# A gated feed-forward kernel on one core: where the ninth group's last mean stands on ScalarE

## The chip, the core and the metric

The kernel runs on one core of one Trainium2 chip. The metric is the device time of one execution in microseconds (us); the median of three executions is given, and one more execution was taken with the hardware profiler. Four engines of the core matter here: TensorE (PE in the profile) does matrix products into accumulation banks, ScalarE (ACT) does activation functions from a loaded table, VectorE (DVE) does element-wise arithmetic, and SyncE (SP) issues the transfers. Every engine works through its own queue of instructions.

## The reference

An attention block without a softmax feeds a gated feed-forward block, all in fp32:

```python
kv  = einsum('bhsd,bhse->bhde', k, v)          # 8 batches, 8 heads, 576 rows, 64 columns
o   = einsum('bhsd,bhde->bhse', q, kv)
x   = o / sqrt(mean(o*o, -1) + 1e-6) * g_norm  # RMS norm per row and head
x   = x.transpose(0, 2, 1, 3).reshape(4608, 512)
h   = x @ w_in                                 # 512 -> 2048
g   = h * erf(log1p(exp(-abs(h))) + maximum(h, 0))   # h * erf(softplus(h))
out = g @ w_out                                # 2048 -> 512
```

## The kernel before, in words

**Groups.** The 4608 rows are worked in nine groups of 512 rows. Groups 0 to 7 are the first 512 rows of each batch; the ninth group (T = 8, `T == B` in the code) collects the last 64 rows of all eight batches, whose attention products were computed along the way and kept in `x_last`. Groups 0 and 1 take a plain fp32 path; from group 2 on every product is made of three products of cut operands ("forms": high part, low part and a mix of both, lines 367 to 390).

**Periods.** From group 2 on the work runs in periods (loop variable `m`, 8 to 36). A period takes a quarter of a group's 2048 hidden columns: `T, b = divmod(m, 4)`. In a period TensorE makes four *hidden products* (function `hidden`, i = 0 to 3, x times a block of w_in) and then four *result products* (function `result`, j = 0 to 3, the gated values of the period before times w_out, added to a running sum `e`). Each of these eight is twelve matmuls of 128x512 (line 434): eight into a bank `n_ps`, then four into a bank `m_ps`. The two banks come from three pairs that go round (`banks`), so product number k writes the pair that product k - 3 used, and has to wait until that one was read.

**What frees a pair.** After a hidden product, ScalarE copies `n_ps` to `h` (line 754), VectorE adds `m_ps` (line 419, called from `add`), and ScalarE takes softplus of the sum (line 756). After a result product, VectorE adds `n_ps` to `e` (line 414) and then `m_ps` (line 419). Each of these also is an instruction in a queue, in the order in which the program is written: the schedule is written out by hand (`manual_schedule`), and no planner moves anything.

**After the four hidden products** ScalarE takes erf of the four softplus tiles in two halves (line 760). Softplus, erf, and the pair Ln and Exp lie in three different tables; a switch is a table load, put in by `exp_ln_table` (line 103), `softplus_table` (line 106) or, for erf, at the activation itself (line 760). After result product 1 VectorE multiplies h by erf's result in two halves (line 772).

**The next group's pieces.** While period `m` runs, it also carries one quarter of the attention of group T + 1, cut into six pieces, and `places` says where each goes: place 0 is ahead of the period's first product, places 1 to 4 follow hidden products 0 to 3, places 5 to 8 follow result products 0 to 3. For the ninth group the six pieces are: nothing, `square` (ScalarE, line 314), nothing, `mean`, `norm` and `split`. `mean` is one fp32 product of 128x512 on TensorE (line 333), then on ScalarE the table of Ln and Exp, Ln (line 340), Exp (341), Square (342) and, if `table` is true, softplus's table again (106). `norm` is three VectorE instructions (348, 351, 360). `split` cuts the normalized tile into its three forms: one ScalarE instruction (385) and two on VectorE (388, 389); they go into `x_forms` of the ninth group, which period 32's first hidden product reads.

The ninth group's four quarters are carried by periods 28 to 31 (T = 7). Periods 28 to 30 have `places = (0, 0, 0, 5, 6, 7)`, so the mean follows result product 0 and stands behind erf on ScalarE. Period 31, the last, has `(0, 0, 0, 2, 4, 5)`: its mean follows hidden product 1.

Of the kernel before, what the change touches and what calls it, by code (L numbers as in the profile page):

```python
# [58 lines left out]
def kernel(  # L59
# [45 lines left out]
    def softplus_table():  # L105
        nc.scalar.preload_act_table_set("softplus")  # L106
# [311 lines left out]
    def add(out_, ps):  # L418
        nc.vector.tensor_tensor(out=out_, in0=ps, in1=out_, op=ALU.add)  # L419
# [44 lines left out]
    NB = FC // BATCH  # L464
# [73 lines left out]
    def load_parts(which, n):  # L538


        pool = w_out_p if which == "out" and len(w_seq["out"]) > BATCH else w_in_p
        for _ in range(n):
            if w_seq[which]:
                key = w_seq[which].pop(0)
                t = pool.tile([P, 3, G], FP32, name=f"w_{which}_parts", tag="w")
                nc.sync.dma_start(out=t, in_=w_kept[key])
                w_now.setdefault(key, []).append(t)
# [124 lines left out]
    def hidden(T, f):  # L672

        w = w_now["in", f].pop(0).rearrange("p i (c f) -> p i c f", c=KC).bitcast(FP32R)
        return product(lambda form, c: w[:, form, c], lambda form, c: x_forms[T][:, form, c])

    def part(h, half):
        return h[:, :, half * 2 * P : half * 2 * P + 2 * P]

    def cut_upper(h, half):  # L680

        t = late_r.tile([P, 3, BATCH, 2 * P], FP32R, name=f"g_forms{half}")
        upper(part(h, half), t[:, 0])
        return t

    def cut_lower(h, half, t):
        lower(part(h, half), *(t[:, i] for i in range(3)))

    def result(T, b, j, g, w):

        ps = product(
            lambda form, f: g[j // 2][:, form, f, j % 2 * P : j % 2 * P + P],
            lambda form, f: w[f][:, form],
        )
        if b == 0:
            es[j] = acc.tile([P, DM], FP32, name="e", tag="e")
            nc.vector.tensor_scalar(
                out=es[j], in0=ps[0], scalar1=SHIFT - 1.0, scalar2=None, op0=ALU.mult
            )
        else:  # L700
            add_scaled(es[j], ps[0], SHIFT - 1.0)
        add(es[j], ps[1])
        if b == NB - 1:
            store(T, j, es.pop(j))
# [5 lines left out]
    for m in range(first_batch, batches + 1):  # L710
        T, b = divmod(m, NB)
        todo = []
        if T + 1 < NG:
            todo = list(attention(T + 1, b))
            if b == 0:
                side = late_r if T % 2 == FIRST % 2 else late
                x_forms[T + 1] = side.tile([P, 3, KC, G], FP32R, name=f"x_forms{(T + 1) % 2}")

        def piece():
            if todo:  # L720
                todo.pop(0)()


        places = (0, 2, 3, 5, 6, 8)
        if T + 1 == B:
            places = (0, 0, 0, 2, 4, 5) if b == NB - 1 else (0, 0, 0, 5, 6, 7)
        elif T + 2 == B and b == NB - 1:
            places = (0, 2, 3, 5, 6, 7)

        def pieces(place):  # L730
            while todo and places[-len(todo)] <= place:
                todo.pop(0)()

        def fetch(place):
            for which in FETCH[place].split():
                load_parts(which, 1)

        pieces(0)
        g, done = g_next, len(g_next)
        g_next = []  # L740
        if m < batches:
            h = wide.tile([P, BATCH, G], FP32, name="h", tag="h")
            s = gate_r.tile([P, BATCH, G], FP32, name="s", tag="s")
        for i in range(BATCH):
            if m < batches:
                n_ps, m_ps = hidden(T, b * BATCH + i)
            fetch(i)
            if i == 0:
                for half in range(done, 2):
                    g.append(cut_upper(old_h, half))  # L750
            if done <= i < 2:
                cut_lower(old_h, i, g[i])
            if m < batches:
                nc.scalar.activation(h[:, i], n_ps, AF.Copy, scale=SHIFT - 1.0)  # L754
                add(h[:, i], m_ps)
                nc.scalar.activation(s[:, i], h[:, i], AF.Softplus)  # L756
            pieces(i + 1)
        if m < batches:
            for i in range(2):
                nc.scalar.activation(part(s, i), part(s, i), AF.Erf)  # L760
            if len(todo) < 3:
                softplus_table()
        T2, b2 = divmod(m - 1, NB)
        w = [w_now["out", b2 * BATCH + f].pop(0).bitcast(FP32R) for f in range(BATCH)]
        for j in range(J):
            result(T2, b2, j, g, w)
            fetch(BATCH + j)
            if j == 1 and m == batches - 1:
                cut_lower(h, 0, g_next[0])

            for half in range(2) if j == 1 and m < batches - 1 else (j,) if j < 2 and m == batches - 1 else ():
                nc.vector.tensor_tensor(  # L772
                    out=part(h, half), in0=part(h, half), in1=part(s, half), op=ALU.mult
                )
            if j == 0 and m == batches - 1:
                g_next.append(cut_upper(h, 0))
            pieces(BATCH + 1 + j)
        old_h = h
# [33 lines left out]
```

## Time and profile before

| | |
|---|---|
| median of 3 executions | 965.39 us (965.13 to 966.09) |
| span of the profiled execution | 966.1 us |
| busy, TensorE | 944.1 us, 98% |
| busy, VectorE | 728.1 us, 75% |
| busy, ScalarE | 616.7 us, 64% |
| table loads at line 106 | 45 of 1283 ns |
| period 31 | from 835.08 us to 862.46 us of the span |

A line of the timeline gives the start in us, the duration in us, the engine, the line of the code, the operation with the tile it writes and those it reads, the number of merged instructions, and in brackets the idle time of the engine before it and who ended it. A line of the table of waits gives the engine and tile that waited, the releaser, the total in us, how often, and the longest. The table of windows gives for a stretch of the span the busy time of each engine with the number of instructions, then the clock that TensorE was granted (1.00 is full), the share of the DMA engines, and GB/s. Durations of matmuls are modelled and overlap the next one; the distance from start to start is the safer measure.

### The profile page before, as it was taken

To read this page: it belongs to the slowest core of one execution; us is meant where nothing else is said; L and a number is where in the kernel's file an instruction comes from. 1 tells how busy PE (TensorE), PEld (TensorE's weight loads), DVE (VectorE), ACT (ScalarE), POOL (GpSimd) and SP (SyncE) were. 2 spreads that over 40 slices of the span, in tenths; PEclk is the share of its full clock that TensorE was granted. 3 is DMA by queue.
4 is the path that set the end of the run, shared out by engine and by line. 5 is a ranking of instruction groups with operands and counts; after the bars stand their busy time and mean duration, and the time that the engine had idled before them with its cause. 6 is when DMAs were issued, how large, how long until landed. Compare 5 with 4: busy or idle time off the path is not lost.

```text
span 966.1 us, 11759 instructions
## 1 busy us (share of the span) xinstructions
PE 944.1 (98%) x4328; PEld 679.6 (70%) x4328; DVE 728.1 (75%) x1036; ACT 616.7 (64%) x824; POOL 2.4 (0%) x10
## 2 busy tenths in 40 slices
PE   6999999999999999999999999999999999989998
PEld 4444444444478887888788878887888787768886
DVE  2979857766277777888888887888787877758667
ACT  3889865686576666666666666666666666665552
POOL 0000000000000000000000000000000000000000
PEclk9999999999999999999999999999999999999999
DMA  9856507889289986998689876987796769756972
GB/s 263 254 163 210 177 1 291 308 317 361 89 302 352 377 290 199 301 382 302 230 270 379 304 282 217 362 334 272 238 353 256 265 228 360 288 211 241 384 275 70
DMA packets 101464, 259.76 MB, mean 269 GB/s; under 512 B 44064, under 2 KB 58400, under 8 KB 101408
## 3 DMA queue, kind: packets, MB, share of 16 engines
q1 hardware_dynamic: 99776, 256.73, 74.7%
q10 hardware_dynamic: 1568, 2.29, 0.8%
q8 instruction: 34, 0.56, 0.2%
q14 instruction: 22, 0.18, 0.0%
q0 software_dynamic: 64, 0.00, 0.0%
HBM read 224.40 MB, written 34.60 MB: 268 GB/s over the span
## 4 chain that ended last, share of the span: by engine, by line
PE 89%; ACT 4%; DVE 3%; DMA 2%; issue 0%; SPq 0%; DVEq 0%
PE n_ps L434 41%; PE m_ps L434 20%; PE o_ps L471 10%; PE h_ps L614 9%; PE se_ps L307 3%; PE kv_ps L279 2%; PE qt_ps L301 2%; DMA w_out_parts<-w_out 1%; DMA v_sb<-in_v_dram 1%; PE ms_ps L333 1%; DMA q_last<-in_q_dram 1%; PE ms_ps L328 1%; PE ms_ps L329 1%; PE kv_ps L306 1%; DVE h L772 0%; ACT w_e L203 0%
## 5 line engine op out<-in xcount | busy, mean ns | idle before, releaser
L434 PE MATMUL n_ps<-x_forms,w_in_parts 128*128 128x512 f32 x896 | 234.2, 403 | 1.3 <-DVE e L414 1.2
L434 PE MATMUL n_ps<-w_out_parts,g_forms 128*128 128x512 f32 x928 | 232.1, 392 | 2.8 <-ACT h L754 2.2
L434 PEld LDWEIGHTS n_ps<-w_out_parts,g_forms 128*128 128x128 f32 x928 | 174.7, 188 | 41.7 <-ACT h L754 2.6
L434 PEld LDWEIGHTS n_ps<-x_forms,w_in_parts 128*128 128x128 f32 x896 | 166.7, 188 | 46.6 <-issue 9.6
L756 ACT ACTIVATE s<-h 128x512 f32<-128x512 f32 x112 | 71.0, 634 | 176.6 <-DVE h L419 176.6
L434 PE MATMUL m_ps<-w_out_parts,g_forms 128*128 128x512 f32 x464 | 125.0, 392 | 0.0
L419 DVE TENSOR_TENSOR h<-m_ps,h 128x512 f32<-128x512 f32 x112 | 77.1, 689 | 61.5 <-ACT h L754 46.2
L434 PE MATMUL m_ps<-x_forms,w_in_parts 128*128 128x512 f32 x448 | 120.1, 390 | 0.0
L614 PE MATMUL h_ps<-xT,w_in_sb 128*128 128x512 f32 x256 | 115.1, 593 | 0.7 <-DVE w_in_sb L228 0.6
L471 PE MATMUL o_ps<-w_out_sb,h_sb 128*128 128x512 f32 x224 | 101.3, 596 | 0.0
L434 PEld LDWEIGHTS m_ps<-w_out_parts,g_forms 128*128 128x128 f32 x464 | 87.7, 189 | 18.3
L434 PEld LDWEIGHTS m_ps<-x_forms,w_in_parts 128*128 128x128 f32 x448 | 84.1, 188 | 17.6
L419 DVE TENSOR_TENSOR e<-m_ps,e 128x512 f32<-128x512 f32 x116 | 80.3, 692 | 18.0 <-PE m_ps L434 11.3
L414 DVE SCALAR_TENSOR_TENSOR e<-n_ps,e 128x512 f32<-128x512 f32 x88 | 60.4, 686 | 43.7 <-PE n_ps L434 43.7
L614 PEld LDWEIGHTS h_ps<-xT,w_in_sb 128*128 128x128 f32 x256 | 48.4, 190 | 60.9 <-issue 56.7
L471 PEld LDWEIGHTS o_ps<-w_out_sb,h_sb 128*128 128x128 f32 x224 | 42.4, 192 | 50.2 <-issue 48.7
L389 DVE SCALAR_TENSOR_TENSOR g_forms<-g_forms 128x1024 fp32r<-128x1024 f32 x58 | 71.1, 1225 | 2.0
L388 DVE TENSOR_TENSOR g_forms<-h,g_forms 128x1024 fp32r<-128x1024 f32 x58 | 70.6, 1218 | 1.5 <-ACT g_forms L385 1.2
L385 ACT ACTIVATE g_forms<-h 128x1024 fp32r<-128x1024 f32 x58 | 59.0, 1059 | 16.7 <-PE m_ps L434 9.8
L754 ACT ACTIVATE h<-n_ps 128x512 f32<-128x512 f32 x112 | 65.5, 584 | 4.1 <-PE n_ps L434 4.1
L772 DVE TENSOR_TENSOR h<-h,s 128x1024 f32<-128x1024 f32 x56 | 66.0, 1219 | 0.7 <-ACT s L760 0.7
L106 ACT ACT_TABLE_LOAD x45 | 57.7, 1283 | 0.8
(84 smaller groups left out, 946.4 us busy)
## 6 DMA issues: line engine op xcount, KB each, us to landing
w_out_parts<-w_out SPq DMA_DIRECT2D x116, 768.0 KB, 7.8
w_in_parts<-w_in SPq DMA_DIRECT2D x112, 768.0 KB, 6.6
w_in<-w_new SPq DMA_DIRECT2D x16, 768.0 KB, 5.5
w_out<-w_new SPq DMA_DIRECT2D x16, 768.0 KB, 6.5
k_sb<-in_k_dram SPq DMA_DIRECT2D x29, 288.0 KB, 5.9
v_sb<-in_v_dram SPq DMA_DIRECT2D x29, 288.0 KB, 6.0
q_sb<-in_q_dram SPq DMA_DIRECT2D x32, 256.0 KB, 5.8
w_raw<-in_moe_w_out_dram SPq DMA_DIRECT2D x8, 1024.0 KB, 5.5
```

The source lines that it names most:

```text
L106: nc.scalar.preload_act_table_set("softplus")
L385: nc.scalar.activation(high, x, AF.Copy, scale=1.0 + 2.0**-13)
L388: nc.vector.tensor_tensor(out=low, in0=x, in1=high.bitcast(FP32), op=ALU.subtract)
L389: nc.vector.scalar_tensor_tensor(out=both, in0=low.bitcast(FP32), scalar=SHIFT, in1=high.bitcast(FP32), op0=ALU.mult, op1=ALU.add,)
L414: nc.vector.scalar_tensor_tensor(out=out_, in0=ps, scalar=scale, in1=out_, op0=ALU.mult, op1=ALU.add)
L419: nc.vector.tensor_tensor(out=out_, in0=ps, in1=out_, op=ALU.add)
L434: nc.tensor.matmul(ps, lhsT=weights(form, k), rhs=moving(form, k), start=(form == forms[0] and k == 0), stop=(form == forms[-1] and k == 3),)
L471: nc.tensor.matmul(o_ps[j], lhsT=g[:, j * P : j * P + P], rhs=w_out_sb[:, f, :], start=(f == 0), stop=last,)
L614: nc.tensor.matmul(plain[i], lhsT=w_in_sb[:, c, i % FC * P : i % FC * P + P], rhs=xT[T][:, c, :], start=(c == 0), stop=(c == KC - 1),)
L754: nc.scalar.activation(h[:, i], n_ps, AF.Copy, scale=SHIFT - 1.0)
L756: nc.scalar.activation(s[:, i], h[:, i], AF.Softplus)
L772: nc.vector.tensor_tensor(out=part(h, half), in0=part(h, half), in1=part(s, half), op=ALU.mult)
```

## The change

In period 31 the ninth group's last mean moves from place 2 to place 4: behind hidden product 3 and its softplus, and just ahead of erf. It is called with `table=False`, so it doesn't load softplus's table at its end, since the next thing ScalarE does is erf, which loads its own. `norm` moves from place 4 to place 5, and `split` from place 5 to place 6, so that they stay behind the mean. Periods 28 to 30 keep their places; the first lines of the diff only write the same choice in another way.

The aim is to take the mean's two table switches from between the softplus of hidden product 1 and the copy of hidden product 2, and to need one table load less.

```diff
         places = (0, 2, 3, 5, 6, 8)
         if T + 1 == B:
-            places = (0, 0, 0, 2, 4, 5) if b == NB - 1 else (0, 0, 0, 5, 6, 7)
+            places = (0, 0, 0, 5, 6, 7)
+            if b == NB - 1:
+
+                places, todo[3] = (0, 0, 0, 4, 5, 6), partial(todo[3], table=False)
         elif T + 2 == B and b == NB - 1:
             places = (0, 2, 3, 5, 6, 7)
```

## The prediction, made before the changed kernel was run

> **What bounds the kernel now.** I read the page's busy times first, then the table of TensorE's waits, then the timeline of period 31. TensorE is the bound, and it waits for little; what it does wait for is listed by releaser:
>
> ```profile
> PE 944.1 (98%) x4328; PEld 679.6 (70%) x4328; DVE 728.1 (75%) x1036; ACT 616.7 (64%) x824; POOL 2.4 (0%) x10
> ```
>
> ```profile
> PE kv_ps L279 <- DMA v_sb<-in_v_dram: 7.5, 3, 5.7
> ...
> PE n_ps L434 <- ACT h L754: 2.2, 1, 2.2
> ...
> PE n_ps L434 <- DVE e L414: 1.2, 2, 0.6
> ```
>
> The longest wait of TensorE in the period loop is one of 2.2 us for a copy on ScalarE (line 754), and the two waits for line 414 are the next. All three are in period 31 and just behind it. The timeline there, with other lines left out:
>
> ```profile
> 845.96 0.63 ACT L756 ACTIVATE s<-h 128x512 f32<-128x512 f32 x1 [1.87 <-DVE h L419]
> ...
> 846.62 1.28 ACT L103 ACT_TABLE_LOAD   x1
> ...
> 849.94 1.28 ACT L106 ACT_TABLE_LOAD   x1
> 851.24 0.60 ACT L754 ACTIVATE h<-n_ps 128x512 f32<-128x512 f32 x1
> ...
> 851.88 2.82 PE L434 MATMUL n_ps<-w_out_parts,g_forms 128*128 128x512 f32 x8 [2.17 <-ACT h L754]
> ...
> 862.46 2.12 PE L434 MATMUL n_ps<-x_forms,w_in_parts 128*128 128x512 f32 x8 [0.51 <-DVE e L414]
> ...
> 866.13 2.11 PE L434 MATMUL n_ps<-x_forms,w_in_parts 128*128 128x512 f32 x8 [0.64 <-DVE e L414]
> ```
>
> The reader sees the mean's block on ScalarE, from 846.62 to 851.22 (4.6 us), and behind it the copy of hidden product 2. Result product 1 is three products after hidden product 2, so it needs that pair of banks; it starts 2.17 us late. The windows show a second cost of the same wait (clock is the third number from the end):
>
> ```profile
> 848.00:852.00 4.00, 1.83 (x9) 1.22 (x8) 0.14 (x1) 3.74 (x5) 0.00 (x0) 1.00 0.98 344
> 852.00:856.00 4.00, 4.00 (x12) 3.15 (x13) 2.75 (x5) 2.64 (x4) 0.00 (x0) 0.63 0.76 314
> ```
>
> TensorE is granted 0.63 of its clock right behind the wait. Finally the late softplus delays erf, the split and the sums on VectorE, which gives the waits at 862.46 and 866.13.
>
> **What the Trainium skill says.** "TensorE: Matmul & The Clock Gate", Part 1 (the HAM clock gate): the array runs at half rate after an idle window and returns to full rate after a busy one, a window being about 3.4 us and free-running. The trace agrees in size: at half rate for a whole window the loss would be 1.7 us, and result product 1 took from 851.88 to 856.21, 4.33 us instead of the 2.72 of its neighbours. It differs on the threshold that the page gives for idleness: here 2.17 us was enough. "ScalarE: Activation LUTs", What ACT_TABLE_LOAD costs: 1283 ns for every set plus about 1380 ns of drain. The trace has 1283 ns, and no drain beside it: the loads at 846.62 and 849.94 are followed by their successors 1.29 and 1.30 us later. I use 1.29. That load from Ln's table straight to erf's isn't in the trace of before; the page's "every set" and the rows of the other switches give one number.
>
> **The change part by part.** I lay the new order out with start-to-start distances from the same timeline.
>
> *TensorE.* Hidden product 1 ends at 840.52, where the mean's product stood; it cost 0.87 us there (hidden product 2's `m_ps` began at 843.21, 1.82 behind a start of 841.39). It isn't removed, only moved behind hidden product 3. So hidden products 2 and 3 start at 840.52 and 843.24 (2.72 each), the mean's product at 845.96, the result products at 846.83, 849.56, 852.28 and 855.00, and period 32 at 857.72, if nothing makes them wait.
>
> *ScalarE, removed.* Two table loads, Ln, Exp and Square leave the place behind softplus 1. The copy of hidden product 2 follows at 846.50 instead of 851.24. Copy to copy is 1.89 (851.24 to 853.13), so its add runs at 847.13 and its softplus at 847.85, the copy of product 3 at 848.39, its add at 849.00 to 849.69 and softplus at 849.72. Result product 1 needs the copy of hidden product 2 by 849.56: it is done by 847.1, 2.4 us early. Result product 2 needs that of product 3 by 852.28, which is done by 849.0. The 2.17 us wait is gone, and with it the half-rate window.
>
> *ScalarE, added ahead of erf.* Table load 850.37, Ln 851.66, Exp 852.38, Square 853.04 to 853.67, erf's load 853.69, two erfs 854.98 to 856.99, softplus's load 857.01, and the split's cut 858.30 to 858.93. One load fewer in all. Before, that cut ran at 859.72, so even behind the mean it is 1.4 us earlier.
>
> *VectorE.* Result product 0's sums finish at 851.16 (850.47 plus 0.69). The norm, now right behind them, waits for Square until 853.70. Queued behind that wait is the sum of result product 1, whose banks period 32's first product needs. Norm takes 2.12 (three starts, 0.73, 0.73, 0.66), so the sum runs at 855.82 and 856.61; done by 856.50 for `n_ps`, and by 857.30 for `m_ps`, before 857.72 and 859.53. Hidden by result products 1 to 3: no cost. Then h times erf, 857.22 (erf's halves end at 856.0 and 857.0), 2.27; the split's line 388 at 859.49 to 860.17 and line 389 at 860.21 to 860.90; result product 2's sum at 860.82 to 861.50.
>
> *New waits.* Period 32's first product reads the ninth group's last forms with its seventh matmul (high) at 857.72 + 6 x 0.227 = 859.08, and its eighth (low) at 859.31. The high form is there at 858.93; the low one at 860.17. Wait: about 0.89 us. Its end moves to 861.34, and the second product needs result product 2's bank, free at 861.50: 0.19 us with the release. Sum: 1.08 us. The mixed form is needed at 861.1 and done at 860.90. After that, copies and sums of period 32 come 1.9 us or more ahead of need. That such a wait costs about its length is seen in period 28, where the same form came late by 0.4 to 0.55 us and the clock stayed at 1.00:
>
> ```profile
> 767.63 0.19 PEld L434 LDWEIGHTS n_ps<-x_forms,w_in_parts 128*128 128x128 f32 x1 [0.55 <-DVE x_forms L388]
> ```
>
> *Sum.* Period 32's third product starts at 861.53 + 2.72 = 864.25, its result products at 869.69. Before, they start at 874.43. Gain: 4.74 us. It agrees with the losses: 2.17, 1.6 of slow clock, 0.51 and 0.64 and some 0.9 of small gaps around them (5.8 from 857.72 + 10.88 = 868.60 to 874.43), less 1.08. Behind that TensorE has no wait to the end of the profile, and the fetches of weights are released by TensorE's own products, so they move with it; the chain hands on the whole gain. 965.39 - 4.74 = 960.65, taken as 960.7.
>
> **Unknown costs.** The new wait of 0.89 lies between 0 (if VectorE reaches the split a slot earlier) and about 2.3 (if the load into erf's table costs the page's 1.38 us of drain); I take 0.89. Half clock behind it costs between 0 and 1.7; I take 0, because two waits of together 1.08 us leave a 3.4 us window two thirds busy. Elsewhere in this trace waits of 0.64, 1.29 and 1.50 us left the clock at 1.00, and one of 1.86 us, at 62, lowered it (0.57 over 64 to 68). This gives 959.6 to about 963.7 at the outer ends.
>
> **The rivals.** *Half rate again* (0.08): the late forms leave TensorE idle long enough to lose the clock in period 32; 960.7 + 1.7 = 962.4. For it: 2.17 us did this in period 31. Against: half that length. *No new wait* (0.10): forms and sums are in time; 960.65 - 1.08 = 959.6. Against it: h times erf stands ahead of the split on VectorE and can't start before erf's second half. *Given back* (0.07): the fetches of w_out set the pace. They land 7.8 us after issue (median), and the last two of period 31 go out when the fourth result product frees their buffers, 13 us ahead of use; against it is that distance. For it: one wait of 0.6 us for w_out in period 29. If all is given back, 965.2. *Slower* (0.03): each of the three table loads between softplus 3 and the split costs the page's full 2.66 instead of 1.29, so the forms come 4.1 us later, TensorE waits 5.2 instead of 1.08 and loses 1.7 to half rate: 5.8 more than forecast, 966.5. Against it: 45 loads of 1.28 us with their successors on their heels.
>
> **How the numbers follow.** The forecast itself has 0.72. It and the first two rivals are faster by over the 1.9 us that can be told; with half of a partly given-back gain, faster has 0.90, same 0.06, slower 0.04. The range for 8 in 10 takes in the no-wait end and the half-clock rival, and some tenths for the timing of before (965.13 to 966.09): 959.3 to 962.8.
>
> **What would show it.** Right: no wait for line 754 in the table of waits, TensorE's clock 1.00 in all of period 31, 44 loads at line 106, a wait for `x_forms` line 388 of 0.6 to 1.2 us at about 859, and period 32's first result product near 869.7. Wrong: a clock below 1 behind 859, waits for DMA in periods 32 to 36, or a gap ahead of period 32's first product, which would mean that the norm's wait held the sum of result product 1 too long.

## The result, and the profile after

| | median, us | lowest to highest | executions |
|---|---|---|---|
| before | 965.57 | 965.13 to 966.09 | 4 |
| changed | 960.53 | 960.31 to 961.31 | 4 |

The ratio is 0.9949, with a 95% interval of 0.9932 to 0.9966: 5.0 us faster. The two profiled spans (966.1 and 958.6 us) differ by more, and part of that has nothing to do with the change. At the first matmul of line 614 (37.88 us in the profile of before, 36.11 in the other) the profiled execution of before was already 1.8 us late, and it lost 1.1 us more behind 64 us of its span, where its TensorE ran at half its clock for 3.4 us and that of the changed kernel did not. So the profiles are compared below over a stretch behind all this.

The page of the changed kernel has one load fewer at line 106 (44 for 45), and ScalarE is busy for 1.6 us less:

```profile
PE 939.5 (98%) x4328; PEld 676.5 (71%) x4328; DVE 728.0 (76%) x1036; ACT 615.1 (64%) x823; POOL 2.4 (0%) x10
...
L106 ACT ACT_TABLE_LOAD x44 | 56.5, 1283 | 0.8
```

In the table of TensorE's waits the copy (line 754, now 757) and line 414 are gone from the list. Two waits for the ninth group's last forms have come:

```profile
PE n_ps L434 <- DVE x_forms L388: 0.7, 1, 0.7
...
PE n_ps L434 <- ACT x_forms L385: 0.7, 1, 0.7
```

The timeline of period 31 and the start of period 32, other lines left out, shows the new order:

```profile
843.13 0.63 ACT L759 ACTIVATE s<-h 128x512 f32<-128x512 f32 x1 [1.88 <-DVE h L419]
843.67 0.58 ACT L757 ACTIVATE h<-n_ps 128x512 f32<-128x512 f32 x1
...
845.81 1.98 PE L434 MATMUL n_ps<-w_out_parts,g_forms 128*128 128x512 f32 x8
...
847.53 1.28 ACT L103 ACT_TABLE_LOAD   x1
...
850.86 1.28 ACT L763 ACT_TABLE_LOAD   x1
850.88 0.69 DVE L348 SCALAR_TENSOR_TENSOR sq<-ms_ps,sq 128x512 f32<-128x512 f32 x1 [2.64 <-ACT sq L342]
...
853.00 0.68 DVE L414 SCALAR_TENSOR_TENSOR e<-n_ps,e 128x512 f32<-128x512 f32 x1
...
853.97 1.52 PE L434 MATMUL n_ps<-x_forms,w_in_parts 128*128 128x512 f32 x6
...
854.39 2.35 DVE L775 TENSOR_TENSOR h<-h,s 128x1024 f32<-128x1024 f32 x2
855.48 0.63 ACT L385 ACTIVATE x_forms<-x 128x512 fp32r<-128x512 f32 x1
...
856.16 0.50 PE L434 MATMUL n_ps<-x_forms,w_in_parts 128*128 128x512 f32 x1 [0.66 <-ACT x_forms L385]
856.66 0.69 DVE L388 TENSOR_TENSOR x_forms<-x,x_forms 128x512 fp32r<-128x512 f32 x1
...
857.40 0.50 PE L434 MATMUL n_ps<-x_forms,w_in_parts 128*128 128x512 f32 x1 [0.74 <-DVE x_forms L388]
```

The copy of hidden product 2 follows softplus 1 within 0.54 us, and result product 1 starts at 845.81 with no wait. The mean's table comes at 847.53 and erf's load at 850.86, with none between. The norm waits 2.64 us on VectorE, and result product 1's sum (853.00) is still in time for period 32's first product (853.97). That product runs six of its matmuls and then waits twice, for the high and for the low form. The clock over the stretch is full (third number from the end):

```profile
848.00:852.00 4.00, 4.00 (x20) 3.30 (x19) 1.33 (x3) 3.91 (x5) 0.00 (x0) 1.00 0.53 215
852.00:856.00 4.00, 3.49 (x16) 2.56 (x14) 3.86 (x6) 3.96 (x5) 0.00 (x0) 1.00 0.38 88
```

**A stretch to compare by.** Softplus 1 of period 31 comes ahead of all that the change moves on ScalarE, and behind period 32's first result product TensorE waits no more in either kernel. Between these two starts lie 28.47 us before (845.96 to 874.43) and 23.89 us after (843.13 to 867.02): 4.58 us of the 5.0 us. Behind that nothing is given back: the two profiled executions are 7.4 us apart at these result products and 7.5 us at the end of their spans. What is over lies within the spread of the executions (1 us in each kernel).

### The profile page after: what moved, and what is told of

Same layout as the page of the kernel before. It is cut to its first block, busy times and chain, and to the rows that moved or that the text cites. A ratio compares the mean times of both kernels' runs of the same rounds, so it can differ in the third digit from the quotient of the medians.

```text
span 958.6 us, 11759 instructions
## 1 busy us (share of the span) xinstructions
PE 939.5 (98%) x4328; PEld 676.5 (71%) x4328; DVE 728.0 (76%) x1036; ACT 615.1 (64%) x823; POOL 2.4 (0%) x10
## 4 chain that ended last, share of the span: by engine, by line
PE 91%; DVE 4%; ACT 3%; DMA 1%; issue 0%; DVEq 0%
PE n_ps L434 42%; PE m_ps L434 21%; PE o_ps L471 10%; PE h_ps L614 9%; PE se_ps L307 3%; PE kv_ps L279 3%; PE qt_ps L301 2%; PE ms_ps L333 1%; PE ms_ps L328 1%; PE ms_ps L329 1%; DMA q_sb<-in_q_dram 1%; DMA v_sb<-in_v_dram 1%; PE kv_ps L306 1%; DVE h L775 0%; ACT w_e L203 0%; ACT w_m L207 0%
```

## The experiments

Each diff is against the changed kernel. "Stretch" is the one just defined, from each kernel's own profile. Kernels with the same time of before were run together on one chip; the before is that of the same chip. A profile shows one execution, and that need not be a typical one: the profiled executions of before (967.84 us) and of "mean only", "place 3" and "behind erf" (966.47, 968.67 and 964.11 us) took 1.5 to 2.5 us longer than the medians. So a stretch and a median can differ by that much.

| kernel | before, us | median, us | ratio (95%) | stretch, us |
|---|---|---|---|---|
| extra load | 965.84 | 961.62 | 0.9964 (0.9951 to 0.9977) | 24.71 |
| norm and split only | 965.84 | 963.26 | 0.9976 (0.9966 to 0.9986) | 26.71 |
| mean only | 965.84 | 964.65 | 0.9989 (0.9981 to 0.9997) | 27.05 |
| mean in idle time | 965.84 | 959.72 | 0.9942 (0.9925 to 0.9959) | 22.00 |
| place 3 | 966.30 | 966.13 | 0.9996 (0.9986 to 1.0006) | 29.14 |
| behind erf | 966.30 | 962.58 | 0.9958 (0.9942 to 0.9975) | 26.31 |
| changed kernel, again | 966.59 | 961.32 | 0.9948 (0.9937 to 0.9960) | 23.91 |
| mean in idle time, again | 966.59 | 959.47 | 0.9923 (0.9911 to 0.9935) | 22.00 |

### Is it the load saved, or the place?

```diff
-                places, todo[3] = (0, 0, 0, 4, 5, 6), partial(todo[3], table=False)
+                places = (0, 0, 0, 4, 5, 6)
```

> The changed kernel, but the mean at place 4 loads softplus's table at its end again, and erf's load follows it: one load of 1.29 us more between softplus 3 and erf. Theory (the gain comes from the copy of hidden product 2 no longer standing behind the mean; what is left is the wait for the late forms): erf, the product with erf and the forms come 1.29 us later, TensorE waits 1.3 us more at the start of period 32, so about 961.8 us, or up to 963.5 us if the longer wait of some 2 us halves the clock for a window. No wait for the copy on ScalarE. Rival (the gain comes from the load saved on ScalarE): the time goes back to before, about 965.5 us.

Measured: 961.62 us, 4.2 us under before. The extra load stands at 851.24 in the timeline of ScalarE, and the load of erf follows at once:

```profile
851.24 1.28 ACT L106 ACT_TABLE_LOAD   x1
852.52 1.28 ACT L763 ACT_TABLE_LOAD   x1
```

TensorE's wait for the high form grows from 0.7 to 1.8 us and that for the low form shrinks from 0.7 to 0.2; the stretch is 0.82 us longer than that of the changed kernel, not the 1.29 us of the expectation. In the changed kernel the high form is done at 856.11 and VectorE takes it up at 856.66, when it is through with h times erf; here VectorE waits for the form, so these 0.55 us of slack take up a part of the load. The place brings most of the gain. The load saved brings 0.8 us by the stretch and 0.8 to 1.1 by the medians, whose intervals overlap.

### Are norm and split only followers?

The mean's new place with the old places of norm and split, and the reverse:

```diff
-                places, todo[3] = (0, 0, 0, 4, 5, 6), partial(todo[3], table=False)
+                places, todo[3] = (0, 0, 0, 4, 4, 5), partial(todo[3], table=False)
```

> The mean at place 4 without softplus's load, as in the changed kernel, but norm at place 4 and split at place 5, as before. Theory: norm now holds VectorE from softplus 3's add until Square, ahead of result product 0's sum, and the split holds it ahead of result product 1's sum, so result product 3 waits 1.5 us for a bank, period 32's first product 1.8 us and the second 1 us; 3.2 to 3.7 us over the changed kernel, 963.7 to 964.2 us. Rival (the mean's place alone brings the gain, norm and split only follow): 960.5 us.

Measured: 964.65 us, 1.2 us under before. In its timeline the norm holds VectorE for 4 us ahead of result product 0's sum, and result product 3 waits for it:

```profile
853.70 0.69 DVE L348 SCALAR_TENSOR_TENSOR sq<-ms_ps,sq 128x512 f32<-128x512 f32 x1 [4.03 <-ACT sq L342]
...
855.82 0.68 DVE L414 SCALAR_TENSOR_TENSOR e<-n_ps,e 128x512 f32<-128x512 f32 x1
```

```profile
856.56 3.56 PE L434 MATMUL n_ps<-w_out_parts,g_forms 128*128 128x512 f32 x8 [2.27 <-DVE e L414]
```

Eight matmuls that take 1.98 elsewhere take 3.56 behind this wait: the clock fell again. Period 32's first product then has no wait and the second one of 0.63 us, where 1.8 and 1 us were expected. The time is half a microsecond over the expected range, but that range was counted from another run of the changed kernel: against the before of each run it meant 1.4 to 1.9 us of gain, and 1.2 (0.3 to 1.8) was measured. The half clock doesn't explain what is missing: two of the thirteen executions had a mean granted clock of 1.000, and they took 964.06 and 964.65 us.

```diff
-                places, todo[3] = (0, 0, 0, 4, 5, 6), partial(todo[3], table=False)
+                places = (0, 0, 0, 2, 5, 6)
```

> The kernel before, but norm and split of period 31 at places 5 and 6; the mean stays at place 2 with both its loads. Theory: the wait of 2.2 us for the copy of hidden product 2 stays, and the half clock behind it; but the sum of result product 1 no longer stands behind the split's wait on VectorE, so the two waits for line 414 go, about 1.4 us: 964.1 us. Rival (the new places of norm and split are what brings the gain): 960.5 us. Rival (only the mean matters): 965.5 us.

Measured: 963.26 us, 2.6 us under before (1.4 to 3.3 by the interval), with the wait for the copy still there (3.03 us in its profile) and none for line 414. The expectation had 1.4 us of gain; the stretch has 1.76. The two halves together bring 3.8 us by the medians and 3.2 by the stretch, less than both at once (5.0 and 4.58): with one of them missing, VectorE's queue or ScalarE's still holds the banks.

### Is the half clock a cost of its own?

```diff
-                places, todo[3] = (0, 0, 0, 4, 5, 6), partial(todo[3], table=False)
+                places = (0, 0, 0, 3, 4, 5)
```

> The kernel before, with period 31's mean one place later (3), with both loads, norm at 4 and split at 5. The copy of hidden product 3 stands behind the mean instead of that of product 2. Theory (from the late softplus 3 on, ScalarE and VectorE run as before, and they set when period 32 begins): TensorE waits 1.4 us for the copy and 0.7 us for line 414 instead of 2.2 us in one piece, its clock stays at 1.00, and yet period 32's first product begins when it did, since the sum of result product 1 stands behind the split: 965.5 us, no gain. Rival (the half clock is a cost of its own): 1.6 to 1.7 us less than before, 963.9 us.

Measured: 966.13 us beside 966.30: no difference. The timeline of TensorE, with only the products that waited:

```profile
853.93 2.11 PE L434 MATMUL n_ps<-w_out_parts,g_forms 128*128 128x512 f32 x8 [2.20 <-ACT h L757]
...
857.37 2.12 PE L434 MATMUL n_ps<-w_out_parts,g_forms 128*128 128x512 f32 x8 [0.41 <-DVE e L414]
...
862.65 3.15 PE L434 MATMUL n_ps<-x_forms,w_in_parts 128*128 128x512 f32 x8 [2.26 <-DVE e L414]
```

The windows behind the first and behind the third of these waits:

```profile
853.90:857.30 3.40, 3.03 (x12) 2.17 (x12) 3.31 (x5) 2.63 (x3) 0.00 (x0) 1.00 0.01 4
862.60:867.00 4.40, 4.35 (x12) 3.45 (x13) 4.19 (x6) 2.31 (x3) 0.00 (x0) 0.61 0.15 63
```

Behind the copy TensorE runs at its full clock here, where before ran at half. It gains nothing by it: it comes to period 32 earlier and waits 2.26 us for result product 1's sum, which stands on VectorE behind the split. (The expectation had waits of 1.4 and 0.7 us, and a clock that stays full.) Period 32 begins 16.53 us after softplus 1 (846.12 to 862.65); in the kernel before it was 16.50 (845.96 to 862.46). So in the kernel before the half clock was covered by the chain over ScalarE and VectorE. In this profile, the slowest of the kernel's fourteen executions, it falls later, in period 32, where the stretch shows it (29.14). The medians can't tell where it fell in the others, so the answer rests on the two starts of period 32, not on them.

With VectorE's chain out of the way the half clock does cost its time. In the kernel with norm and split only, TensorE has no other wait between the late copy (848.82) and the start of period 32 (858.73). These three result products take 9.91 us instead of 3 x 2.72 = 8.16, and the clock (third number from the end) is halved for 3.4 us from 849.90 on:

```profile
849.90:853.31 3.41, 3.41 (x10) 2.64 (x9) 2.53 (x4) 2.64 (x4) 0.00 (x0) 0.50 0.04 16
```

### Does it matter on which side of erf the mean stands?

```diff
-                places, todo[3] = (0, 0, 0, 4, 5, 6), partial(todo[3], table=False)
+                pass
```

Period 31 then has the places of periods 28 to 30.

> Period 31 with the places of periods 28 to 30: mean behind erf at place 5, norm at 6, split at 7; the same number of table loads as the changed kernel. Theory: no wait for the copy either, but the split's cut comes 0.8 us later and the low form 1.1 us later than in the changed kernel, since erf, Ln's table, Ln, Exp, Square and softplus's table all stand ahead of the norm: 961.5 us. Rival (the order of mean and erf makes no difference as long as the mean is out of the hidden products): 960.5 us. Rival (the load saved is the gain): 960.5 us too.

Measured: 962.58 us, 3.7 us under before, so 1.3 to 1.6 us behind the changed kernel (5.0 and 5.3 under its own). The two were not run together and their intervals overlap, so the medians alone don't decide it. It has as many table loads as the changed kernel. The waits for the forms are longer (2.5 us in all for 1.4), and in the profile the clock fell behind them:

```profile
858.39 0.50 PE L434 MATMUL n_ps<-x_forms,w_in_parts 128*128 128x512 f32 x1 [1.67 <-ACT x_forms L385]
859.73 0.80 PE L434 MATMUL n_ps<-x_forms,w_in_parts 128*128 128x512 f32 x1 [0.83 <-DVE x_forms L388]
```

### Can the wait that is left be removed?

ScalarE sits idle for 3.6 us between the copy of hidden product 0 and its softplus, since VectorE is busy with the forms of the period before. In the kernel before:

```profile
842.97 0.64 ACT L756 ACTIVATE s<-h 128x512 f32<-128x512 f32 x1 [3.57 <-DVE h L419]
```

The mean's 4.6 us nearly fit there, with both loads:

```diff
-                places, todo[3] = (0, 0, 0, 4, 5, 6), partial(todo[3], table=False)
+                places = (0, 0, 0, 1, 2, 3)
...
                 add(h[:, i], m_ps)
+                if i == 0 and T + 1 == B and b == NB - 1:
+                    todo.pop(0)()
                 nc.scalar.activation(s[:, i], h[:, i], AF.Softplus)
```

> The mean of period 31 between the copy of hidden product 0 and its softplus, where ScalarE sat idle for 3.6 us, with both loads; norm at place 2, split at place 3. Theory (in the changed kernel only the late forms are left of the cost, 2.1 us in its profile): softplus 0 comes about 1.1 us later, which nothing waits for; forms are ready before period 32, no wait of TensorE from period 30 to the end; 2.1 us under the changed kernel, 958.4 us, though it has one table load more. Rival (table loads and ScalarE's work set the time): slower than the changed kernel, 961.8 us or more.

Measured: 959.72 us, 6.1 us under before: 1.1 us more gain than the changed kernel's 5.0, half of what was expected. Since the two had not been run together and their intervals overlap, both were run once more on one chip:

> The changed kernel beside the kernel before and the next one, on one chip. Theory: its gain over before is the one that the two profiles show between softplus 1 of period 31 and the first result product of period 32, 4.6 us: 4.4 to 5.2 us under before.

> The mean of period 31 between the copy of hidden product 0 and its softplus, again, on one chip with the changed kernel. Theory: the same stretch was 1.9 us shorter in its profile (22.0 against 23.9 us), so 1.5 to 2.2 us under the changed kernel and 6.1 to 7 us under before. Rival: the wait for the late forms only hid other waits, and the two take the same time.

Measured: 961.32 and 959.47 us beside 966.59. The changed kernel is 5.3 us under before, the other 7.1 us, each a tenth beyond the expected range, and the other is 1.85 us under the changed kernel, within the range. All five of its executions (958.38 to 959.88) are shorter than the shortest of the changed kernel (960.35). The timeline of its ScalarE (second run), from the copy of hidden product 0 on:

```profile
835.80 0.58 ACT L757 ACTIVATE h<-n_ps 128x512 f32<-128x512 f32 x1
836.39 1.28 ACT L103 ACT_TABLE_LOAD   x1
...
839.72 1.28 ACT L106 ACT_TABLE_LOAD   x1
841.01 0.64 ACT L761 ACTIVATE s<-h 128x512 f32<-128x512 f32 x1
...
842.94 0.64 ACT L761 ACTIVATE s<-h 128x512 f32<-128x512 f32 x1 [0.81 <-DVE h L419]
...
846.19 0.62 ACT L385 ACTIVATE x_forms<-x 128x512 fp32r<-128x512 f32 x1
```

Softplus 1 still waits for VectorE (0.81 us), as it did in the changed kernel (1.88 us), and it comes as long after period 31's start (11.78 us for 11.79), so the mean held nobody up; the split's cut runs at 846.19, 7.9 us ahead of period 32's start at 854.06. TensorE has no wait from 360 us of the span to its end. This version has one load more than the changed kernel and is the fastest of all.

## Why the prediction was right

The forecast was 960.7 us and the measurement 960.53. That the two agree to 0.2 us is in part luck: before came out at 965.57 us instead of 965.39, and the gain at 5.0 us (5.3 in the second run) instead of 4.74. By its steps:

- **The copy's wait goes.** Right. The copy comes 0.54 us after softplus 1, as laid out, and result product 1 doesn't wait. The extra-load kernel, which keeps the place and gives back the load, keeps 4.2 us of gain.
- **The new order on ScalarE.** Right to 0.01 us: the split's cut was laid out 12.34 us after softplus 1 (858.30 less 845.96) and came 12.35 after it (855.48 less 843.13). The load from Ln's table straight to erf's, which no row of before showed, took 1.28 us without anything beside it, the lower of the two values weighed.
- **VectorE's queue.** Right. The norm's wait was laid out as 2.54 us and is 2.64; the low form's start was laid out 13.53 us after softplus 1 and came 13.53 after it. The mean-only kernel shows what moving norm and split behind the sums was for.
- **The new wait.** Right in place; too small by half on TensorE's side. Laid out as 0.89 for the low form and 0.19 for a bank, 1.08 us in all, with the high form in time. Measured, TensorE waited for both forms (0.66 and 0.74 us), and period 32's four hidden products took 13.05 us (853.97 to 867.02) instead of 4 x 2.72 = 10.88: 2.17 us lost. The reason is not the forms, which came on time after softplus 1, but that TensorE came 0.9 us earlier: softplus 1 lies 10.88 us behind period 31's start in the profile of before and 11.79 in that of the changed kernel. The other profiles have 11.6 to 11.85, so the one that I had taken this distance from is the odd one. It has a wait of 0.6 us for w_out in period 29 that the profile of the changed kernel doesn't have; that this is the whole cause isn't shown. In the sum it cancels: behind softplus 1 the forms set the pace, and a TensorE that comes earlier waits longer for them.
- **The clock.** Right that it stays full in period 31. The waits for the forms in the two profiles of the changed kernel left it at 1.00, and the last section gives a reason. But the cross-check of the sum is no second proof. It lists TensorE's losses up to 874.43, with 0.9 us of small gaps as the remainder, so it must agree with the schedule that it was taken from. Read as a list of gains it misleads: the place-3 kernel shows that the 1.6 us of half clock alone would have brought nothing, since the waits for line 414 were shorter by what it took. The forecast itself came from the two schedules.
- **Handed on to the end.** Right: no wait of TensorE behind period 32's second product in the profile after.
- **The sum.** 4.74 us was laid out for the stretch, 4.58 measured in it, 5.0 between the medians.

Of the rivals, "no new wait" isn't what happened, but the mean-in-idle kernel shows it can be had, and that it is worth 1.85 us. "Half rate again" is seen in the profiles of the mean-only and behind-erf kernels, whose waits are longer. "Given back" and "slower" did not come: the profile of the changed kernel has no wait for w_out, and its new load took 1.28 us. One slip in the chances: the forecast and the first two rivals alone add up to the 0.90 that is given to "faster", so half of the 0.07 of "given back" would make it 0.93 or 0.94.

## What to carry to other kernels

Where TensorE is the bound and waits once, follow the wait to the engine that released it, and look at what stood ahead of the releasing instruction in that engine's queue: here 4.6 us of work whose result was needed more than ten microseconds later. Move it to a place where that engine is idle anyway, not only to one where it does less harm; the number of table loads mattered less than where they stood. When several waits and a slow clock lie behind one another, don't add them up as gains: lay out both schedules from a common start, and check which chain sets the next start.

## What the runs showed of the hardware

**When a wait halves the clock.** Its length alone doesn't decide it. Waits of 2.17 us (before) and 2.27 us (mean only) were followed by half rate, one of 2.20 us (place 3) was not, and the wait of 1.9 us that all kernels have near 62 us was followed by half rate in five of the ten profiles and not in the others; of the two profiles of the mean-in-idle kernel, the same program, one has it and one doesn't.

The Trainium skill ("TensorE: Matmul & The Clock Gate", Part 1) says that the clock is set by free-running windows of about 3.4 us, and that half rate comes after an idle one. In these traces every stretch at half rate up to 950 us lasted 3.41 us, and in the place-3 profile the two begin at 64.71 and 863.43 us, 234 times 3.413 us apart. Counted back in such steps from 863.43, a border between windows falls at 853.19, inside the wait of 2.20 us (851.73 to 853.93); the wait of 2.26 us (860.39 to 862.65) lies in one window. Window before and window behind, for each of the two:

```profile
849.78:853.19 3.41, 1.95 (x9) 1.29 (x7) 0.00 (x0) 3.32 (x5) 0.00 (x0) 1.00 0.94 389
853.19:856.60 3.41, 2.67 (x12) 2.17 (x12) 2.62 (x4) 2.61 (x5) 0.00 (x0) 1.00 0.02 9
...
860.02:863.43 3.41, 1.15 (x5) 0.67 (x4) 2.71 (x5) 0.52 (x1) 0.00 (x0) 1.00 0.73 222
863.43:866.84 3.41, 3.41 (x9) 2.65 (x8) 3.31 (x4) 2.15 (x3) 0.00 (x0) 0.50 0.02 9
```

TensorE is idle for 1.46 us in the first window, and full clock follows; it is idle for 2.26 us in the third, and half rate follows. Cut in this way, the ten profiles have ten windows with 1.70 us or more of idle TensorE up to 950 us of the span, and half rate follows each; no window with less (1.66 us is the most) is followed by it. So here an idle share of about one half was enough, where the page speaks of an idle window. In the last 10 us of the mean-only kernel one window with 1.9 us was not followed by half rate. The two waits of the changed kernel come to 1.4 us, which is under the mark wherever the windows fall. No run was made to try this by itself.

**Two table loads in a row**, softplus's and erf's, took 1.28 and 1.30 us from start to start (extra load), with no further time for the engine to empty.
